# A single pair's projection on four array tiles, two fillers fewer, and the last output tile in two halves

## Chip, cores, metric

One core of one Trainium2 chip. The metric is the device time of one execution in microseconds (us). "us" of a record or a stretch is read from the profile of one execution; its clock starts with the span, which is some 1.7 us shorter than the device time.

## The reference, cut to what matters

```python
# q, k, v: (4, 8, 768, 64); proj: (64, 6)
q_bits = (einsum('bhsd,dk->bhsk', q, proj) > 0);  k_bits likewise
mask = bucket(q_bits)[:, :, :, None] == bucket(k_bits)[:, :, None, :]
scores = where(mask, q @ k.T / 8, -1e9);  attn = softmax(scores)
x = (attn @ v) laid out as (3072, 512)
out = (silu(x @ w_in)) @ w_out          # w_in (512, 2048), w_out (2048, 512)
```

The mask compares six sign bits of q and k. The kernel puts these bits, as extra rows of the contraction, under q and k, so that one matmul gives the score and, for unequal bits, a large negative term.

## The kernel before

Heads are worked in pairs. For pair 0 and pair 1 the projection (six random directions for each of q and k) is made for one pair alone; the later ones are made for two pairs at once, on the four 32-column tiles of the array.

```python
def proj_unit(*pairs):
    tiles = [(p, n) for p in pairs for n in range(2)]        # 2 tiles for one pair, 4 for two
    w = 32 * len(tiles)
    ...
    for c0, c1 in ((0, 512), (512, S)):
        for c, (p, n) in enumerate(tiles):
            nc.tensor.matmul(bp[32 * c : 32 * c + 32, 0 : c1 - c0], pw,
                             qk32[p][:, n * S + c0 : n * S + c1], start=True, stop=True)
    # VectorE: threshold to 0.5 or -0.5, one operation for each of the two banks

def bits_unit(pairs, i, par):      # VectorE: bits to where the scores' matmuls read them
    for n in range(2):             # q, then k: copies of 13 x 768, fp16
        ...
```

The start, with filler matmuls (`warm_up`) that keep TensorE busy while it would wait:

```python
t_unit(0, 0)
t_unit(0, 1, warm=4)       # 4 fillers between the transposes of q and of k
t_unit(0, 2)
warm_up(3)
cast_unit(0, 0)            # GpSimd: q and k to fp16 for the even head
cast_unit(0, 1)            # ScalarE: for the odd head
v_unit(0)                  # GpSimd: v of two heads to fp16, and its sums
proj_unit(0)
warm_up(9)
bits_unit((0,), 0, 0)      # for the even head (qka)
bits_unit((0,), 0, 1)      # for the odd head (qkb)
...
for p in range(NPAIR):
    plan(2 * NU * (p + 1) + 3, lambda p=p: x_unit(p))     # transposes of a pair's output
```

At the end, the second layer makes an output tile of 128 x 512 from 16 matmuls; VectorE halves it into SBUF and one transfer stores it:

```python
for ft in range(4 * part, 4 * part + 4):
    nc.tensor.matmul(o2[tt], g[ci][:, ft, ct * P : (ct + 1) * P], w_out16[:, ft, :], ...)
if part == 3:
    nc.vector.tensor_scalar(out=osb, in0=o2[tt], scalar1=0.5, scalar2=None, op0=ALU.mult)
    nc.sync.dma_start(out=dst[:, tt, :], in_=osb)
```

The softmax here doesn't subtract the row's maximum and nothing guards it: scores larger than these inputs give would overflow.

## Time and profile before

| | before |
|---|---|
| device time, median of 3 | 331.89 us |
| span of the profiled run | 330.2 us |
| TensorE busy, and its part of the chain that ended last | 98%, 90% |
| first projection (pair 0) on the chain | 1.51 us |
| first exponential of the scores | 12.40 us |
| last eviction, start | 326.52 us |

A chain line reads "start, duration, what": at each step the work that released the next one. The lines themselves are in the prediction below.

### The profile page before, as it was taken

What the parts mean: (1) busy time and instruction counts of PE and PEld (TensorE: products, weight loads), DVE (VectorE), ACT (ScalarE), POOL (GpSimd) and SP (SyncE); (2) the same over time, 40 slices, a digit from 0 to 9 for tenths busy, and PEclk for the clock granted to TensorE, in tenths of its full rate; (3) what the DMA queues carried; (4) which work ended last, traced back from release to release, by engine and by line L of the source; (5) the groups of instructions that cost most, each with busy time, mean ns of one, the idle gap of its engine ahead of it and who ended that gap; (6) DMA issues with size and microseconds to landing.
All of it is one profiled execution on the core that took longest, in us unless ns stands there. A gap on an engine that the chain in (4) does not pass through costs nothing.

```text
span 330.2 us, 7269 instructions
## 1 busy us (share of the span) xinstructions
PE 323.1 (98%) x2903; PEld 196.2 (59%) x2903; DVE 163.6 (50%) x335; ACT 226.6 (69%) x424; POOL 111.3 (34%) x177
## 2 busy tenths in 40 slices
PE   7999999999999999999999999999999999999995
PEld 4566645664786555665686655665576555448442
DVE  4586627348752181356953173345864222577311
ACT  2787989997996654897897645699798556267000
POOL 5689999329003570038303191034700000000000
PEclk9999999999999999999999999999999999999999
DMA  8999999960000381590000092220000010100021
GB/s 181 238 250 219 230 218 202 246 167 0 2 0 34 79 178 68 174 239 4 0 2 3 32 218 70 90 71 3 3 0 2 32 66 35 64 0 3 32 95 66
DMA packets 60259, 29.84 MB, mean 90 GB/s; under 512 B 50496, under 2 KB 56640, under 8 KB 60224
## 3 DMA queue, kind: packets, MB, share of 16 engines
q1 hardware_dynamic: 57472, 25.17, 31.8%
q0 software_dynamic: 2752, 4.20, 7.2%
q8 instruction: 23, 0.38, 0.5%
q14 instruction: 12, 0.10, 0.1%
HBM read 27.27 MB, written 6.29 MB: 102 GB/s over the span
## 4 chain that ended last, share of the span: by engine, by line
PE 90%; DVE 5%; ACT 2%; DMA 1%; issue 0%; ACTq 0%
PE o_ps L320 25%; PE h_ps L303 24%; PE s_ps L247 17%; PE o_ps L266 11%; PE tp_ps L162 6%; PE bp_ps L204 4%; DVE qka L224 2%; PE o_ps L261 2%; DMA q_sb<-in_q_dram 1%; PE xt_ps L286 1%; ACT u L250 1%; PE warm_ps L95 1%; DVE g L309 1%; DVE qkb L221 1%; DVE xT L288 1%; DVE qkb L224 1%
## 5 line engine op out<-in xcount | busy, mean ns | idle before, releaser
L250 ACT ACTIVATE u<-s_ps 128x512 f16<-128x512 f32 x288 | 160.2, 622 | 48.8 <-PE s_ps L247 48.4
L303 PE MATMUL h_ps<-xT,win 128*128 128x512 f16 (+1 forms) x512 | 95.3, 326 | 0.7 <-DVE xT L288 0.3
L266 PEld LDWEIGHTS <-u 128*128 128x128 f16 x1152 | 69.9, 97 | 42.4 <-ACT u L250 10.1
L320 PE MATMUL o_ps<-wout,g 128*128 128x512 f16 x384 | 94.4, 379 | 0.0
L309 DVE SCALAR_TENSOR_TENSOR g<-th,h_ps 128x512 f16<-128x512 f32 x96 | 65.7, 686 | 47.5 <-ACT th L307 47.3
L266 PE MATMUL o_ps<-vv,u 128*128 128x65 f16 x1152 | 82.4, 194 | 0.6 <-ACT u L250 0.3
L307 ACT ACTIVATE th<-h_ps 128x512 f32<-128x512 f32 x96 | 57.5, 599 | 24.9 <-PE h_ps L303 22.4
L303 PEld LDWEIGHTS <-win 128*128 128x128 f16 x512 | 49.5, 98 | 30.1 <-issue 3.0
L176 POOL TENSOR_SCALAR qka<-qk 64x1536 f16<-64x1536 f32 x16 | 23.4, 1463 | 118.5 <-ACT qk L166 115.0
L320 PEld LDWEIGHTS <-g 128*128 128x128 f16 x384 | 37.1, 98 | 35.6 <-issue 0.8
L247 PE MATMUL s_ps<-qkb 128*128 128x512 f16 x192 | 53.1, 326 | 0.0
L247 PE MATMUL s_ps<-qka 71*128 71x512 f16 x192 | 52.7, 327 | 0.0
L325 DVE TENSOR_SCALAR osb<-o_ps 128x512 f32<-128x512 f32 x24 | 16.6, 690 | 59.1 <-PE o_ps L320 59.1
L166 ACT COPY qk<-tp_ps 128x512 f32<-128x512 f32 x38 | 24.5, 645 | 5.4 <-PE tp_ps L162 5.4
L176 POOL TENSOR_SCALAR qkb<-qk 64x1536 f16<-64x1536 f32 x15 | 22.0, 1468 | 1.2
L275 DVE RECIPROCAL rec<-o_ps 128x6 f32<-128x6 f32 x32 | 6.1, 190 | 29.6 <-PE o_ps L266 29.6
L187 POOL TENSOR_TENSOR vsa<-v_sb 128x192 f32<-128x192 f32 x32 | 20.2, 632 | 0.0
L276 DVE TENSOR_TENSOR x_pr<-o_ps,rec 128x384 f16<-128x384 f32 x32 | 17.8, 557 | 1.1
L185 POOL CAST vv<-v_sb 128x384 f16<-128x384 f32 x32 | 17.8, 555 | 0.5
L224 DVE COPY qka<-bits 13x768 f16<-13x768 f16 x32 | 16.4, 514 | 0.7
L162 PE MATMUL tp_ps<-ident,q_sb 128*128 128x128 f32 x96 | 16.0, 279 | 0.4 <-DMA q_sb<-in_q_dram 0.4
L247 PEld LDWEIGHTS <-qka 71*128 71x128 f16 x192 | 15.5, 97 | 0.5 <-POOL vsb L189 0.3
(44 smaller groups left out, 189.8 us busy)
## 6 DMA issues: line engine op xcount, KB each, us to landing
q_sb<-in_q_dram SPq DMA_DIRECT2D x16, 384.0 KB, 6.5
k_sb<-in_k_dram SPq DMA_DIRECT2D x16, 384.0 KB, 6.9
v_sb<-in_v_dram SPq DMA_DIRECT2D x16, 384.0 KB, 5.3
out_dram<-osb SPq DMA_DIRECT2D x24, 256.0 KB, 2.0
win<-in_moe_w_in_dram POOLq DMA_DIRECT2D x4, 512.0 KB, 7.9
wout<-in_moe_w_out_dram POOLq DMA_DIRECT2D x4, 512.0 KB, 11.9
pw<-in_proj_dram POOLq DMA_DIRECT2D x2, 1.5 KB, 4.3
```

The lines of the kernel that those rows point to most:

```text
L162: nc.tensor.transpose(tp[:, j * P : (j + 1) * P], src[:, t].rearrange("p h d -> p (h d)"), ident)
L166: nc.scalar.copy(dst, tp)
L176: nc.gpsimd.tensor_scalar(out=dst[rows, :], in0=qk32[p][rows, :], scalar1=CS, scalar2=1.0, op0=ALU.mult, op1=ALU.mult)
L187: nc.gpsimd.tensor_tensor(out=sa, in0=src[:, 0:3], in1=src[:, 3:6], op=ALU.add)
L224: nc.vector.tensor_copy(out=dst, in_=bits[pairs][r, :])
L247: nc.tensor.matmul(sp[:, o0 : o0 + n], t[rows, S + jt * P : S + (jt + 1) * P], t[rows, c0 : c0 + n], start=True, stop=True)
L250: nc.scalar.activation(out=u, in_=sp, func=AF.Exp, scale=ESC)
L266: nc.tensor.matmul(o_ps[h][:, c0 // P + i, :], u[:, o0 + i * P : o0 + (i + 1) * P], vv[:, jt, :], start=False, stop=True, skip_group_check ...
L303: nc.tensor.matmul(hp[:, j, :], w_in16[dt][:, ft * P : (ft + 1) * P], xT[4 * b + dt][:, c0 : c0 + n], start=(dt == 0), stop=(dt == NDT - 1))
L307: nc.scalar.activation(out=th, in_=hp, func=AF.Tanh, scale=0.5)
L309: nc.vector.scalar_tensor_tensor(out=g[ci][:, grp * f : (grp + 1) * f, :], in0=th, scalar=1.0, in1=hp, op0=ALU.add, op1=ALU.mult)
L320: nc.tensor.matmul(o2[tt], g[ci][:, ft, ct * P : (ct + 1) * P], w_out16[:, ft, :], start=(ft == 0), stop=(ft == NFT - 1))
```

## The change

Its intent: spread the projection of a single pair over four array tiles (both halves of the sequence, for q and k), so that TensorE streams 384 columns instead of 768; take two fillers away ahead of k; and make the last output tile in two column halves, so that less is left to evict and to store behind the last matmul.

```diff
-        tiles = [(p, n) for p in pairs for n in range(2)]
-        chunks = ((0, 512), (512, S))
+        if len(pairs) == 1:
+            HS = S // 2
+            tiles = [(pairs[0], n, i * HS, i * HS, HS) for i in range(2) for n in range(2)]
+            chunks = [(0, HS, tiles)]
+        else: ...                        # two pairs: as before
 ...
     def bits_unit(pairs, i, par):
-        for n in range(2):               # 2 copies of 13 x 768
+        if len(pairs) == 1:              # 4 copies of 13 x 384
+            moves = [(2 * i + n, n, i * (S // 2), S // 2) for i in range(2) for n in range(2)]
+        else:
+            moves = [(2 * i + n, n, 0, S) for n in range(2)]
 ...
+        def mm2_last():
+            for i in range(2):
+                c = slice(i * DMODEL // 2, (i + 1) * DMODEL // 2)
+                op = ps.tile([P, DMODEL // 2], F32, tag="m", name="o2_ps", bufs=3)
+                for ft in range(NFT):
+                    nc.tensor.matmul(op, g[1][:, ft, P : 2 * P], w_out16[:, ft, c], ...)
+                ... # halve it, store it
 ...
-    t_unit(0, 1, warm=4)
+    t_unit(0, 1, warm=2)
```

More of the change, by code (lines that the diff above doesn't have):

```diff
@@ L194, in proj_unit @@
     def proj_unit(*pairs):
-        tiles = [(p, n) for p in pairs for n in range(2)]
-        w = 32 * len(tiles)
         bt = btp.tile([P, S], F16, tag="bits", name="bits")
-        chunks = ((0, 512), (512, S))
+        if len(pairs) == 1:
[3 more added lines that the diff above has]
+        else:
+            chunks = [(c0, n, [(p, m, 0, c0, n) for p in pairs for m in range(2)])
+                      for c0, n in ((0, 512), (512, S - 512))]
         bps = []
-        for c0, c1 in chunks:
+        for c0, w, tiles in chunks:
             bp = ps.tile([P, 512], F32, tag="m", name="bp_ps", bufs=3)
-            for c, (p, n) in enumerate(tiles):
-                nc.tensor.matmul(bp[32 * c : 32 * c + 32, 0 : c1 - c0], pw,
-                                 qk32[p][:, n * S + c0 : n * S + c1],
+            for c, (p, n, _, x0, w) in enumerate(tiles):
+                nc.tensor.matmul(bp[32 * c : 32 * c + 32, 0:w], pw,
+                                 qk32[p][:, n * S + x0 : n * S + x0 + w],
                                  start=True, stop=True)
             bps.append(bp)
-        for bp, (c0, c1) in zip(bps, chunks):
-            nc.vector.tensor_scalar(out=bt[0:w, c0:c1], in0=bp[0:w, 0 : c1 - c0],
-                                    scalar1=sc[0:w, 0:1], scalar2=sc[0:w, 1:2],
+        for bp, (c0, w, _) in zip(bps, chunks):
+            nc.vector.tensor_scalar(out=bt[:, c0 : c0 + w], in0=bp[:, 0:w],
+                                    scalar1=sc[:, 0:1], scalar2=sc[:, 1:2],
                                     op0=ALU.is_gt, op1=ALU.subtract)
@@ L215, in bits_unit @@
         p = pairs[i]
-        for n in range(2):
-            r = slice(32 * (2 * i + n), 32 * (2 * i + n) + NR)
-            t, r0 = ((QKA[p % NSL], 64), (QKB[p % NSL], 0))[par]
-            dst = t[r0 : r0 + NR, n * S : (n + 1) * S]
+        t, r0 = ((QKA[p % NSL], 64), (QKB[p % NSL], 0))[par]
+        if len(pairs) == 1:
+            moves = [(2 * i + n, n, i * (S // 2), S // 2) for i in range(2) for n in range(2)]
+        else:
+            moves = [(2 * i + n, n, 0, S) for n in range(2)]
+        for c, n, x0, w in moves:
+            r = slice(32 * c, 32 * c + NR)
+            dst = t[r0 : r0 + NR, n * S + x0 : n * S + x0 + w]
             if n == 1 and par == 1:
-                nc.vector.tensor_scalar(out=dst, in0=bits[pairs][r, :],
+                nc.vector.tensor_scalar(out=dst, in0=bits[pairs][r, 0:w],
                                         scalar1=sc[r, 2:3], scalar2=None, op0=ALU.mult)
             else:
-                nc.vector.tensor_copy(out=dst, in_=bits[pairs][r, :])
+                nc.vector.tensor_copy(out=dst, in_=bits[pairs][r, 0:w])
     NU = 9
@@ L313, in moe_units @@
         o2 = {}
+        def mm2_last():
[3 more added lines that the diff above has]
+                for ft in range(NFT):
+                    nc.tensor.matmul(op, g[1][:, ft, P : 2 * P], w_out16[:, ft, c],
+                                     start=(ft == 0), stop=(ft == NFT - 1))
+                osb = ops.tile([P, DMODEL // 2], F32, tag="osb", name="osb")
+                nc.vector.tensor_scalar(out=osb, in0=op, scalar1=0.5, scalar2=None,
+                                        op0=ALU.mult)
+                dst = out[b * S : (b + 1) * S, c].rearrange("(p t) n -> p t n", p=P)
+                nc.sync.dma_start(out=dst[:, NJ - 1, :], in_=osb)
         def mm2(tt, part):
@@ L334, in moe_units @@
         for tt in range(NJ):
+            if b == B - 1 and tt == NJ - 1:
+                units.append(mm2_last)
+                break
             for part in range(4):
```

## The prediction

> **What bounds the kernel now.** I read the page first, then the chain of waits over the first 21 us, then time-ordered views of the vector engine around the first projection and of the last 5 us. The page:
>
> ```profile
> PE 323.1 (98%) x2903; PEld 196.2 (59%) x2903; DVE 163.6 (50%) x335; ACT 226.6 (69%) x424; POOL 111.3 (34%) x177
> PEclk9999999999999999999999999999999999999999
> PE 90%; DVE 5%; ACT 2%; DMA 1%; issue 0%; ACTq 0%
> ```
>
> TensorE holds 90% of the chain that ended last and is busy 98% of the span, at full clock. So a change pays where it takes TensorE work off this chain, or shortens the two ends, where TensorE waits for a load or has nothing left to do. The chain from the start, in order of time (start us, us, what):
>
> ```profile
> 0.75 4.26 DMA q_sb<-in_q_dram
> 5.00 0.14 issue
> 5.14 1.28 PE tp_ps L162 x6
> 6.42 0.86 PE warm_ps L95 x4
> 7.28 0.65 PE tp_ps L162 x6
> 7.93 0.65 PE warm_ps L95 x3
> 8.58 1.51 PE bp_ps L204 x8
> 10.09 2.05 PE warm_ps L95 x9
> 12.13 0.24 PE s_ps L247
> ...
> 17.86 1.41 PE bp_ps L204 x8
> ```
>
> All three places of the change are on or next to it: four fillers between the transposes of q and k, the projection of pair 0, and that of pair 1. Note that 9 fillers follow the first projection: the first scores wait for them, not only for the bits. The vector engine there:
>
> ```profile
> 7.53 0.69 DVE L168 COPY qk<-tp_ps 128x512 f32<-128x512 f32 x1 [2.89 <-PE tp_ps L162]
> 9.69 1.25 DVE L209 TENSOR_SCALAR bits<-bp_ps,sc 64x512 f16<-64x512 f32 x2 [1.47 <-PE bp_ps L204]
> 10.98 0.86 DVE L224 COPY qka<-bits 13x768 f16<-13x768 f16 x2
> ```
>
> The bits that the first scores need are in place at 10.98 + 0.86 = 11.84, just before the fillers end at 12.13. The end of the kernel:
>
> ```profile
> 326.10 0.38 PE L320 MATMUL o_ps<-wout,g 128*128 128x512 f16 x1
> 326.52 0.69 DVE L325 TENSOR_SCALAR osb<-o_ps 128x512 f32<-128x512 f32 x1 [2.76 <-PE o_ps L320]
> 327.23 0.33 SPq L328 DMA_DIRECT2D out_dram<-osb  x1
> ```
>
> After the last matmul come 0.69 us of eviction and, from the issue at 327.23, 2.0 us to the landing (median of the output stores), all exposed.
>
> **What the Trainium skill says.** "TensorE: Matmul & The Clock Gate", section "Part 3: Packing small matmuls", says that matmuls on different 32-column strips of the array run concurrently, so that a pack costs about one matmul's duration plus some 4 ns per tile. The trace agrees: a projection of two pairs (four strips, 16 records) takes 1.43 us on the chain at 47.23, one of a single pair (two strips, 8 records) 1.41 us at 17.86. Two strips lie idle in the single one. "VectorE: DVE Perf Modes", section "The TRN2 errata", says that a VectorE instruction has a fixed cost besides its per-element time, so many small tiles pay it many times. The trace agrees: 802 ns for 512 columns and 527 for 256 in the same threshold operation give (802 - 527)/256 = 1.07 ns a column, so 527 - 275 = 252 ns fixed. "DMA: Bandwidth & Descriptors", section "Anatomy of one DMA", puts some 2.0 us of fixed setup and completion on a transfer (on another issue path); here the whole 256 KB store lands in 2.0 us, so the fixed part is smaller, but the split still shortens only the moving of the data.
>
> **The change part by part.**
>
> *Two fillers fewer ahead of k.* Four take 0.86 us, so two take 0.43 and TensorE would be free at 6.42 + 0.43 = 6.85. But the weight load of k's first transpose shows a wait of 0.18 us that ends with the landing of k, and it starts at 6.97. The chain has its transposes from 7.28, though the first one's record starts at 7.12 already (the chain counts only what follows the last filler's end). If it starts right after the weight load, as q's did (load 5.11, matmul 5.14), it starts at 7.00. So of the 0.43 us taken away, 0.12 at most is won, and none if the load needs its 0.14 us first. I take 0.07; k's landing takes the place of the fillers.
>
> *Projection of pair 0.* Before: the two strips run 512 columns, then 256, each in two passes (two records a matmul): 768 columns in 1.51 us. After: four strips run 384 columns at once. The stream is half as long. [...]The streaming part: a 512-column pass takes 0.43 us (the second pair of weight loads of this unit start 8.97, the third 9.39), so 768 columns in two passes take 0.43 x 2 x 1.5 = 1.29 us, and 384 take 0.64. Saved on TensorE 0.64 of 1.51, leaving about 0.87. The 9 fillers move up with it.
> The bits, meanwhile: the threshold can start only when the whole bank is done, some 0.9 to 1.0 us after the projection starts at 8.58 (now 1.1, behind the 512-column half), so at about 9.5; then one operation of 384 columns, 252 + 384 x 1.07 = 663 ns, in place of two that take 1.25 together: done at 10.2 instead of 10.94. Then four copies of 384 columns where there were two of 768. A plain copy of 768 took 0.36 (qkb) to 0.66 us (pair 1's qka); in pair 0 two took 0.86. If half of a 0.43 us copy is fixed, a copy of 384 takes 0.32, and the four 1.3 us, against 0.86. Bits in place at 11.5, three of the four (enough for the first score) at 11.2. The fillers end at 12.13 - 0.64 = 11.49. So the bits arrive about as the fillers end: the bound remains TensorE, with little room. I subtract 0.05 for this race. Pair 0: 0.64 - 0.05 = 0.59 us.
>
> *Projection of pair 1.* The same halving inside a stretch where TensorE is the bound and ScalarE waits for it (1.22 us idle before its exponential at 19.98): 1.41 becomes 0.77, 0.64 us saved. Its bits are needed only by the scores at 22.52, with qka's copies done at 20.20 + 1.33 = 21.53, about 1 us of room. The copies become four; at worst 0.45 us each, or 0.5 us more in all, the threshold gives 0.6 back, and the score comes 0.64 earlier relative to the projection's start. The room shrinks but holds.
>
> *Last output tile in halves.* 16 matmuls of 512 columns become 32 of 256. The weight loads double to 32, at 98 ns each in their record, and the 256-column matmuls of the first layer (272 ns a record, pipelined) show that this pace holds: in the stretch from 285.45 to 305.76, 64 of 512 and 64 of 256 take 20.3 us; with 0.216 a wide one, 64 x 0.216 = 13.8, leaving 6.5/64 = 0.10 a narrow one. So TensorE needs the same 3.45 us. The first half's eviction and store lie under the second half's 1.7 us of matmuls. The exposed eviction drops from 690 ns to 690 - 256 x 1.07 = about 420: 0.27 us. The exposed store is 128 KB instead of 256. Its data phase is estimated: the stores' data move at about 344 GB/s in the slice view of the last 5 us, so 128 KB less is 0.38 us; [...]I take 0.30. Sum 0.57.
>
> Sum: 0.07 + 0.59 + 0.64 + 0.57 = 1.87 us, 331.89 - 1.87 = 330.0.
>
> **The rivals.**
> *The early gain is swallowed later*, by a wait with its own clock. For: the DMA engines run at 80 to 90% until about 66 us, GpSimd at 90% from 16 to 41. Against: after the first q no load is on the chain; k of pair 1 is issued at 4.79 and used at 14.76, with 6.9 us the median to landing, 3 us of room. GpSimd's cast of pair 2 is done at 26.4, used at 33.6. If it came true, only the tail's 0.57 and something of the rest would stay: 331.0 or so.
> *The bits become the bound of the first scores.* For: twice as many copies, each with its fixed cost, beside GpSimd, and pair 1's copies of 768 took 0.66 each. If the four take 0.5 each, the bits come at 12.2 and nearly all of pair 0's 0.59 is gone: 330.6. Against: the copies of pair 0 averaged 0.43 and only three are needed.
> *Four strips at once don't keep up with single-pair data*, or the fewer fillers cost clock: speaking against, the two-pair unit at 1.43 us for four strips, and a removed span of 0.43 us of which TensorE idles only about 0.15, while 3 more fillers follow at once. A half-rate clock for 3 us would add some 1.5 us and cancel the gain: 331.5.
>
> **Range and chances.** The sure part is 0.64 + 0.57, so I'd be surprised above 331.0; with k early and a faster store it could reach 329.5. 8 in 10: 329.5 to 330.8. Over 2% would need 6.6 us, over three times all of it; slower by 2% would need a lost clock over tens of microseconds. Faster 0.01, same 0.98, slower 0.01.
>
> **What would show it.** In the changed profile: k's transposes start near 7.0 to 7.1 in the records with a short gap behind the fillers; the two single projections take 0.8 to 0.9 and 0.75 to 0.8 us on the chain; the first exponential starts at 11.6 to 11.8 instead of 12.40, and fillers, not bits, precede it; one 128x384 threshold takes about 0.66 us; from 21 us on everything lies 1.2 to 1.4 us earlier and the distance holds to the last layer; the last eviction takes about 0.42 us and the last store lands some 1.7 us after issue. It is wrong if the distance shrinks on the way, if the chain shows the vector engine ahead of the first scores, or if the clock drops.

## The result

| | before | after |
|---|---|---|
| median (lowest to highest), 6 runs each | 332.05 (331.83 to 332.36) | 331.64 (331.43 to 331.92) |
| ratio | | 0.9987, 95% interval 0.9974 to 1.0000 |
| span of the profiled run | 330.2 | 329.9 |

A ratio here is the mean time of one kernel's runs over that of the other's of the same rounds, so it isn't quite the ratio of the medians. 0.4 us came of the 1.87 that were predicted, and the interval reaches 1. The page of the changed kernel looks the same as before, with one hint in its line of the chain by engine: VectorE's part has grown.

```profile
PE 89%; DVE 6%; ACT 2%; DMA 2%; issue 1%; SPq 0%; ACTq 0%
```

The chain of waits of the changed kernel over the first scores (here and below, lines of "issue" of 0.05 us and less are left out of a chain):

```profile
7.03 0.87 PE tp_ps L162 x6
7.91 0.65 PE warm_ps L95 x3
8.55 0.91 PE bp_ps L209 x8
9.48 0.69 DVE bits L214
...
10.20 0.57 DVE qka L234
10.78 0.55 DVE qka L234
...
11.36 0.37 DVE qka L234
11.77 0.39 PE s_ps L257
```

The projection is down from 1.51 to 0.91 us as predicted. But behind it the chain has left the fillers and runs through VectorE: three copies of 384 columns take 0.57, 0.55 and 0.37 us. Before, two copies of 768 took 0.86 in all. Half as many columns made the single copy no shorter.

The same chain from the projection of pair 1 on:

```profile
17.64 0.83 PE bp_ps L209 x8
...
19.20 0.78 DVE qka L234
20.00 0.55 DVE qka L234
...
23.34 1.20 DVE qk L168 x2
24.54 0.11 DVE rec L285
24.68 0.57 DVE x_pr L286
25.29 0.51 PE xt_ps L296 x6
```

The projection takes 0.83 instead of 1.41 us. Then the chain stays on VectorE for 6.8 us: threshold, eight bit copies, two evictions of transposes, and the division of head 1 (x_pr). Only then can TensorE transpose pair 0's output (xt_ps). In the kernel before, the division (a line of the time-ordered view) was done at 24.24, and TensorE came to the transposes (a line of the chain) 1.4 us later:

```profile
23.68 0.56 DVE L276 TENSOR_TENSOR x_pr<-o_ps,rec 128x384 f16<-128x384 f32 x1
25.67 0.33 PE xt_ps L286 x6
```

The changed kernel's list of waits in the stretch from 20 to 28 us puts numbers to it: engine, line, what it waited for, us, times, longest.

```profile
ACT u L260 <- PE s_ps L257: 0.9, 1, 0.9
PEld L296 <- DVE x_pr L286: 0.7, 1, 0.7
PE xt_ps L296 <- DVE x_pr L286: 0.5, 1, 0.5
```

And the end, in order of time:

```profile
326.36 0.42 DVE L334 TENSOR_SCALAR osb<-o_ps 128x256 f32<-128x256 f32 x1 [1.32 <-PE o_ps L331]
326.81 0.33 SPq L337 DMA_DIRECT2D out_dram<-osb  x1
```

The last eviction is 0.27 us shorter (0.42 instead of 0.69), and the stores of 128 KB land 1.7 us after issue (2.0 before, for 256 KB). 326.81 + 1.7 = 328.51, and the span ends at 329.9: 1.4 us later. Before, 327.23 + 2.0 = 329.23 and 330.2: 1.0 us. So something like 0.4 us has appeared behind the landing.

To see where time goes without the noise of the launch, I cut each trace into stretches by the starts of records: from the first projection matmul to the first exponential of the scores, from that to the last such exponential, and from there to the start of the last record.

| kernel | projection to first exponential | first to last exponential | last exponential to end |
|---|---|---|---|
| before | 3.89 | 267.37 | 50.33 |
| after | 3.70 | 267.38 | 50.24 |

0.19 us won at pair 0 (0.59 predicted), nothing at pair 1 (0.64 predicted), 0.09 at the end (0.57 predicted). Over all runs below, a stretch that an edit doesn't touch repeats within 0.05 us; this is what makes parts of some tenths of a microsecond legible, while the device times scatter by a microsecond and more.

### The profile page after: what moved, and what is told of

The parts are those of the page before. It is cut to its first block, busy times and chain, and to the rows that moved or that the text cites. A ratio compares the mean times of both kernels' runs of the same rounds, so it can differ in the third digit from the quotient of the medians.

```text
span 329.9 us, 7309 instructions
## 1 busy us (share of the span) xinstructions
PE 321.7 (98%) x2917; PEld 196.4 (60%) x2917; DVE 166.5 (50%) x342; ACT 226.6 (69%) x424; POOL 111.0 (34%) x177
## 4 chain that ended last, share of the span: by engine, by line
PE 89%; DVE 6%; ACT 2%; DMA 2%; issue 1%; SPq 0%; ACTq 0%
PE o_ps L344 24%; PE h_ps L313 24%; PE s_ps L257 17%; PE o_ps L276 11%; PE tp_ps L162 6%; PE bp_ps L209 4%; DVE qka L234 2%; DMA k_sb<-in_k_dram 2%; PE o_ps L271 1%; ACT u L260 1%; PE xt_ps L296 1%; PE o_ps L331 1%; DVE g L319 1%; DVE qkb L231 1%; DVE qkb L234 1%; DVE xT L298 1%
## 5 line engine op out<-in xcount | busy, mean ns | idle before, releaser
L344 PE MATMUL o_ps<-wout,g 128*128 128x512 f16 x368 | 91.0, 379 | 0.0
L344 PEld LDWEIGHTS <-g 128*128 128x128 f16 x368 | 35.5, 98 | 33.7 <-issue 0.8
L349 DVE TENSOR_SCALAR osb<-o_ps 128x512 f32<-128x512 f32 x23 | 15.9, 690 | 56.3 <-PE o_ps L344 56.3
L234 DVE COPY qka<-bits 13x768 f16<-13x768 f16 (+1 forms) x36 | 17.9, 496 | 0.8
L162 PE MATMUL tp_ps<-ident,k_sb 128*128 128x128 f32 x96 | 15.6, 273 | 0.6 <-DMA k_sb<-in_k_dram 0.6
```

The lines of the kernel that those rows point to most:

```text
L162: nc.tensor.transpose(tp[:, j * P : (j + 1) * P], src[:, t].rearrange("p h d -> p (h d)"), ident)
L234: nc.vector.tensor_copy(out=dst, in_=bits[pairs][r, 0:w])
```

## The experiments

My theory had three parts. One: GpSimd's work beside the bit copies lengthens them, and the bits become the bound of the first scores. Two: the eight copies of pair 1 hold up VectorE's queue, and TensorE waits for the division behind them. Three: the end has closing waits (the last records of the sync engine, each a wait for two semaphores, the counters by which transfers and engines tell that they are done), and what they cost depends on which semaphore the last store uses. The rivals are in the expectations. Each run was timed in five rounds, with runs of the kernel before in between.

### One transfer more, nothing else

```diff
-        nc.sync.dma_start(
-            out=t, in_=v[b, h0 : h0 + 2].rearrange("h (p t) d -> p h (t d)", p=P))
+        for hh in ((0, 2),) if p != 12 else ((0, 1), (1, 2)):
+            nc.sync.dma_start(
+                out=t[:, hh[0] : hh[1]],
+                in_=v[b, h0 + hh[0] : h0 + hh[1]].rearrange("h (p t) d -> p h (t d)", p=P))
```

> The kernel before with one load (values of pair 12) issued as two transfers of half the size; nothing else. The transfers on the sync queue become 73 instead of 72, and the last store takes the first of the eight semaphores in turn instead of the eighth. Theory (closing waits): the sync engine waits for the eight semaphores in a fixed order at the end, some 0.06 us each, and seven of them now come after the landing of the last store, so 0.4 us is added at the end: about 332.4 against 332.0, and the profile shows the span longer by 0.4 us with the last store landing at the same time. Rival (the tail of the changed kernel lost its gain elsewhere, in the matmuls or the store): no change, within 0.1 us.

Measured: 332.50 us (332.16 to 332.65) against 331.71, ratio 1.0018 (1.0006 to 1.0030). The three stretches: 3.89, 267.34, 50.78. The last is 0.45 us longer than before, and nothing else moved. The rival has fallen: this kernel's last eviction and store are the old ones. The sync engine's records at the end show the mechanism. Each row is one closing wait, with the two semaphores named in it and the time on the profile's clock at which it was over; the left column is the kernel before, the right one the changed kernel:

```
before                               after
327.23 store, semaphore 118          326.81 store, semaphore 101
327.61 wait 113, 112                 327.19 wait 113, 112
327.68 wait 101, 111                 328.53 wait 101, 111   <- the last store has landed
327.75 wait 103, 110                 328.59 wait 103, 110
327.81 wait 104, 109                 328.66 wait 104, 109
327.87 wait 105, 108                 328.72 wait 105, 108
327.93 wait 114, 107                 328.78 wait 114, 107
328.00 wait 116, 106                 328.84 wait 116, 106
328.05 wait 117, 100                 328.90 wait 117, 100
329.26 wait 118, 115   <- landed     328.96 wait 118, 115
```

Eight semaphores serve the sync queue's transfers in turn. With 72 transfers the last one has the semaphore that is waited for last, and the other waits run while it is in flight. With 73 it has the first of the eight, and seven waits of some 0.06 us come after its landing: 328.96 - 328.53 = 0.43 us. The run with one transfer more shows the same in its own records: 329.55 - 329.12 = 0.43 us.

### The halves alone

The last output tile in two halves, as in the change, and nothing else (73 transfers).

> The kernel before with only the last output tile in two column halves (73 transfers). Theory (closing waits): eviction 0.27 us and store 0.31 us shorter, 0.43 us given back in the closing waits: 0.15 us faster, 331.9 against 332.05. Rival (the prediction's own sum): 0.58 us faster.

Measured: 331.64 us (331.59 to 332.35) against 331.71, ratio 1.0000 (0.9988 to 1.0013): the times can't tell 0.1 from 0. The stretches can: 3.89, 267.34, 50.24, so 0.10 us won and not 0.58.

### The halves with one load fewer

```diff
     def load_v(p):
         b, h0 = p // 4, 2 * (p % 4)
+        if p == 13:
+            return
+        if p == 12:
+            t = vld.tile([P, 4, NJ * D], F32, tag="ldv4", name="v_sb", bufs=1)
+            nc.sync.dma_start(
+                out=t, in_=v[b, h0 : h0 + 4].rearrange("h (p t) d -> p h (t d)", p=P))
+            v_sb[12], v_sb[13] = t[:, 0:2], t[:, 2:4]
+            return
```

> The same, and the values of pairs 12 and 13 loaded by one transfer instead of two, so that the transfers number 72 and the last half store has the eighth semaphore again. Theory (closing waits): the whole 0.58 us is there, 331.45 against 332.05, and 0.43 less than the kernel with the halves alone. Rival: the same time as with the halves alone.

Measured: 331.48 us (331.11 to 331.81) against 331.71, ratio 0.9989 (0.9977 to 1.0001). The stretches: 3.89, 267.32, 49.80. The end is 0.53 us shorter than before and 0.44 shorter than with the halves alone. So the prediction's 0.57 for eviction and store was there all along; a wait behind the landing ate it. The rival has fallen.

This run happened to show the fillers too. The clock of TensorE came up at 7.06 us (the trace's record of the granted clock; in the other runs between 4.36 and 6.94). Until then matmuls take about twice as long: in the kernel before, where it came up at 6.04, the first seven fillers took 3.15 us, the nine behind the projection 2.05. So here the four fillers ahead of k began at the low clock and took 1.17 us instead of 0.86. Chain of this run, with four fillers:

```profile
5.05 1.51 PE tp_ps L170 x6
6.57 1.17 PE warm_ps L103 x4
7.74 0.66 PE tp_ps L170 x6
```

### Pair 0 alone

The change's fillers and its four-tile projection for pair 0; pair 1 and the last tile as before.

```diff
-        if len(pairs) == 1:        # after, in proj_unit and in bits_unit
+        if pairs == (0,):
```

> The changed kernel with its two fillers fewer and its four-strip projection for pair 0 only; pair 1 in two strips and the last tile whole, as before. Theory (the copies of 384 columns are no shorter than those of 768 while GpSimd works, and the first scores wait for them): the first exponential at 12.2 instead of 12.4, 0.2 us faster in all. Rival (the prediction): the fillers are the bound, the first exponential at 11.7 to 11.8, 0.6 us faster.

Measured: 331.65 us (331.35 to 332.63) against 331.71, ratio 0.9999 (0.9986 to 1.0012): within the noise. The stretches: 3.70, 267.34, 50.32. So the 0.19 us at the first scores belong to pair 0, and no more than that; the first exponential stood at 12.15 us. The clock came up almost as late here (6.94), but with two fillers:

```profile
4.99 1.51 PE tp_ps L162 x6
6.50 0.71 PE warm_ps L95 x2
7.22 0.65 PE tp_ps L162 x6
```

The first transpose of k starts at 7.05 in its own record, against 7.57 with four fillers and the late clock. (k had landed at 6.71 and 6.61: TensorE came late in both.)

### Pair 1 alone

As the last, with `pairs == (1,)` and four fillers.

> The kernel before with the four-strip projection for pair 1 alone. Theory (vector engine queue): the projection is 0.6 us shorter, but eight bit copies instead of four hold up the vector engine, the division of head 1 comes late behind them, TensorE waits for it at the transposes of pair 0's output, and the stretch from the first exponential to the last stays at 267.3 us. Rival (the prediction): that stretch is 0.6 us shorter.

Measured: 331.86 us (331.61 to 332.65) against 332.03, ratio 0.9997 (0.9981 to 1.0014). The stretches: 3.89, 267.39, 50.33. The middle one stays at its 267.37. The exponentials show where the gain was and went: the 13th starts 6.95 us behind the first (7.58 before), so 0.63 us had been won there; the 25th starts 14.05 behind it (14.03 before), and it is gone.

### Pair 1 alone, transposes of pair 0's output later

```diff
-        plan(2 * NU * (p + 1) + 3, lambda p=p: x_unit(p))
+        plan(2 * NU * (p + 1) + (7 if p == 0 else 3), lambda p=p: x_unit(p))
```

> The same, with the transposes of pair 0's output planned four windows later (25 instead of 21), by when the vector engine has caught up. Theory (vector engine queue): the wait of TensorE before these transposes goes, and the stretch from the first exponential to the last becomes 266.7 us, 0.6 less. Rival (another bound in this stretch, ScalarE or a bank of the transposes waiting for its copy): it stays at 267.3.

Measured: 331.05 us (330.85 to 331.96) against 332.03, ratio 0.9976 (0.9958 to 0.9994). The stretches: 3.90, 266.73, 50.33. The 0.64 us of pair 1 are back in full. The wait for x_pr is missing from this run's list of waits; the transposes now follow TensorE's own work without a gap:

```profile
26.30 0.21 PE s_ps L258
26.52 0.34 PE xt_ps L297 x6
```

Nothing else bounds this stretch: the eight copies are as slow as before, but nobody waits for them.

### Pair 0, with GpSimd still during the copies

What spoke for GpSimd in the first place were its records in the changed kernel beside the copies:

```profile
10.15 0.51 POOL L185 CAST vv<-v_sb 128x384 f16<-128x384 f32 x1
10.62 0.59 POOL L187 TENSOR_TENSOR vsa<-v_sb 128x192 f32<-128x192 f32 x1
11.29 0.32 POOL L189 TENSOR_TENSOR vsb<-vsa 128x64 f32<-128x64 f32 x1
```

These end at 10.66, 11.21 and 11.61. The first three copies end at 10.77, 11.33 and 11.73: each 0.11 or 0.12 us after the GpSimd operation that ran when it was issued. (All sixteen bit operations of pairs 0 and 1 in this trace end 0.10 to 0.12 us after such an operation; in the kernel before, the six copies of 768 columns end 0.21 or 0.22 after.) The Trainium skill names a cause that fits, on a page that the prediction did not use: "SBUF — State Buffer", section "Who interferes with whom", says that VectorE and GpSimd share a pair of SBUF ports, that copies in the fast two-port modes need it, and that whoever issues first keeps it for the whole instruction. No trace names the mode of a copy or the port; what a run can show is whether GpSimd's work is the cause. The experiment, against the run of pair 0 alone:

```diff
-        if p == 0 and par == 1:        # cast_unit: which half ScalarE takes
+        if p == 0 and par == 0:
 ...
     cast_unit(0, 0)
-    cast_unit(0, 1)
-    v_unit(0)
+    v_unit(0, (0,))
     proj_unit(0)
     warm_up(9)
     bits_unit((0,), 0, 0)
+    hold = cst.tile([P, 1], F16, name="hold")
+    nc.gpsimd.tensor_copy(out=hold[64:77, :],
+                          in_=QKA[0][64:77, 2 * S - 1 : 2 * S])   # waits for the 4th copy
+    v_unit(0, (1,))
+    cast_unit(0, 1)
     bits_unit((0,), 0, 1)
```

> The changed kernel's pair 0 and fillers alone (as in the earlier run of these), with GpSimd kept still while the first four bit copies run: its values of head 0 are taken earlier, the cast of q and k for the even head goes to ScalarE, and a one-element operation that waits for the fourth copy goes ahead of the rest of GpSimd's work. Theory (GpSimd in the way of the copies): each of the four copies takes some 0.37 us, like those that ran beside GpSimd's small operations, the third is done before the fillers end, and from the start of the projection to the first exponential it takes 3.2 to 3.3 us instead of 3.70 (before: 3.89). Rival (a copy of 384 columns from one group of partitions to another takes 0.55 us by itself): the first two copies stay at 0.55 and the stretch at 3.70.

Measured: 331.19 us (331.01 to 332.67) against 332.03, ratio 0.9980 (0.9961 to 0.9999). The stretches: 3.25, 267.34, 50.35. The first is 0.64 us shorter than before: what the prediction had reckoned for the projection, without the 0.05 that it took off. In order of time on VectorE:

```profile
9.97 1.08 DVE L235 COPY qka<-bits 13x384 f16<-13x384 f16 x4
11.09 0.25 DVE L235 COPY qkb<-bits 13x384 f16<-13x384 f16 x1
...
11.69 0.45 DVE L235 COPY qkb<-bits 13x384 f16<-13x384 f16 x1
```

Four copies in 1.08 us, 0.25 each in the trace, less even than the 0.37 that I had expected (those had still waited behind small operations). The next plain copy after GpSimd goes on at 11.46 is at 0.45 again. The rival, a copy that is slow by itself, has fallen. On the chain the scores follow the fillers again, as the prediction had it:

```profile
9.20 2.05 PE warm_ps L95 x9
11.25 0.23 PE s_ps L258
```

### All three remedies with the whole change

The change, with GpSimd still, the transposes later, and one load fewer.

> The whole change with the three remedies together: GpSimd still during the first bit copies, the transposes of pair 0's output four windows later, and one load fewer so that the last store has the eighth semaphore. If the three theories hold, against the kernel before: 0.6 us at pair 0, 0.6 at pair 1, 0.53 at the end, and 0 to 0.4 from the fillers depending on when the clock comes up: 1.7 to 2.0 us faster, about 330.0. If one of them is wrong, its part is missing.

Measured: 329.88 us (329.82 to 329.96) against 332.03, ratio 0.9933 (0.9920 to 0.9947). The stretches: 3.25, 266.71, 49.79, so 0.64 + 0.66 + 0.54 = 1.84 us; the rest of the 2.15 between the medians lies ahead of the projection, which starts 0.26 us earlier in the profiled run (k's landing, the clock and the fillers differ from run to run), and in the scatter. Repeated:

> The change with the three remedies once more, as the standard for the next run: 329.9, 2.0 us under the kernel before.

Measured: 329.87 us (329.75 to 330.24) against 332.05, ratio 0.9936 (0.9923 to 0.9950), stretches 3.25, 266.69, 49.81. With the time taken out of the waits, the change gives what was predicted of it.

### The remedies without the change

GpSimd still and the transposes later, in the kernel before.

> The kernel before with the two remedies that touch its own work (GpSimd still during the first bit copies, the transposes of pair 0's output four windows later) and nothing of the change. Theory: in this kernel the fillers are the bound of the first scores and no one waits at the transposes, so both remedies bring nothing: 3.89 us, 267.3 us and 50.3 us for the three stretches, within 0.05. Rival (the remedies are gains by themselves): 0.4 and 0.6 us less.

Measured: 331.57 us (331.46 to 332.45) against 332.05, ratio 0.9991 (0.9977 to 1.0004). The stretches: 3.88, 267.33, 50.33, all as before. In the kernel before nobody waited at these places, so the remedies are no gains of their own. The median is 0.5 us lower, but the interval holds 1 and none of the three stretches carries it; this profiled run's k had merely landed early, and its first transpose stood at 6.64 us. The third remedy, one load fewer, was not tried without the change.

### The fillers alone

`warm=2` for `warm=4` in the kernel before.

> The kernel before with two fillers ahead of k instead of four, nothing else. Theory (the clock decides): the clock comes up at another moment in each run (4.4 to 7.1 us so far); with four fillers a late clock keeps k's transposes back (7.56 at a clock of 7.05), with two they start within 0.1 us of k's landing always. So 0 to 0.5 us, 0.1 to 0.2 on the mean, and the rest of the program as before: 3.89 from the projection to the first exponential, 267.3 to the last, 50.3 to the end. Rival (fewer fillers bring the clock up later): the transposes or the projection run longer than before.

Measured: 331.80 us (331.68 to 332.06) against 332.05, ratio 0.9993 (0.9980 to 1.0005): unclear by time, where 0.1 to 0.2 us was expected. The stretches: 3.89, 267.36, 50.34, untouched. The clock came up at 4.93 here, and transposes, fillers and projection ran no longer than elsewhere, so the rival found no support; but with an early clock two fillers gain nothing either. What they gain is shown only by the late clocks: k's first transpose at 7.57 with four fillers (clock at 7.06), at 7.05 with two (6.94); two more runs with two fillers and the clock at 6.3 to 6.5 had it at 6.79 and 6.86. That two fillers always let it start within 0.1 us of k's landing, as expected, had been contradicted already by the run of pair 0 alone: 7.05 with k landed at 6.71. How often the clock is that late, and so the mean gain, stays open.

### Seven fillers for nine

The mended kernel with `warm_up(7)` for `warm_up(9)` behind the first projection, to see whether the fillers bound the first scores again.

> The same with seven fillers behind the first projection instead of nine. Theory (with GpSimd still, the fillers are the bound of the first scores again; the third copy was done at about 10.76 and the fillers ended at 11.24): the first scores start at 10.8, 0.43 us earlier, and the projection to the first exponential takes 2.8 us instead of 3.25; 0.43 us faster, about 329.45. Rival (the bits or the sum of the values are the bound already): no gain; or the clock falls back: slower.

Measured: 329.62 us (329.55 to 329.70) against 332.05, ratio 0.9927 (0.9914 to 0.9939), and 0.25 us under the mended kernel. First stretch 3.04 instead of 3.25: 0.21 won, half of what I expected. The chain says why:

```profile
10.62 0.26 DVE qka L242
10.92 0.39 PE s_ps L265
```

The fillers were the bound, and with two fewer the bits are: the third copy ends at 10.88, and the scores follow. This is the fastest version measured, 2.4 us under the kernel before by the medians.

## Why the prediction was wrong, point by point

- **What bounds the kernel** was right: TensorE, and both ends. That the change would stay far within 2% was right too.
- **Fillers ahead of k**: 0.07 us expected. The profiled pair of traces gives 0.09 by k's first transpose (7.12 to 7.03 us, though k landed 0.07 later) and 0.03 by the start of the projection. So the size came out about right partly by luck: it depends on k's landing, which the prediction took from one trace, and on when the clock comes up, which it left out.
- **Projection of pair 0 on TensorE**: 0.64 us expected, 0.60 on the chain (1.51 to 0.91), right. The step that failed is "If half of a 0.43 us copy is fixed, a copy of 384 takes 0.32", with "the bits arrive about as the fillers end", for which 0.05 was taken off. The copies took 0.57, 0.55 and 0.37 us, and the race cost 0.45 (3.70 against 3.25 with GpSimd still). The rival "the bits become the bound of the first scores" was the one that came true, and even its figure (0.5 each) was close; it was given too little weight. A copy's duration was taken for a property of the copy. Alone, a copy of 384 columns takes 0.25 us, less than the 0.32 reckoned, and one of 768 takes 0.35 (the run of the remedies without the change). Beside GpSimd each copy waited until an operation of GpSimd was over, which was more than half of the first two copies' 0.57 and 0.55 us; so the time went with the number of copies, which the change doubles, and hardly with their length.
- **Projection of pair 1**: the 0.6 us was won on TensorE (the 13th exponential 0.63 us sooner), and given back. The step that failed is "The room shrinks but holds". It looked at one consumer of the bits, the scores, whose room did hold. The one that waited needs no bits at all: the division of head 1, which stands behind the eight copies in VectorE's queue, and through it the transposes on TensorE. The division had had 1.4 us of room; the eight bit copies took 4.1 us, where four had taken 2.2, and TensorE wanted its result 0.6 us sooner. That GpSimd lengthened these copies too (0.78, 0.55, 0.53 us) is likely, since they end 0.11 us after its operations as at pair 0, but no run kept it still at pair 1.
- **Last tile**: the sum of 0.57 us was right (0.53 once the closing waits lie before the landing), though the store's part partly by luck: the 0.30 came from 0.38 by a deduction that no run shows, and the landings differ by 0.31. The step that failed is one that isn't in the prediction: it let the end of the span follow the landing by a fixed time. A 73rd transfer moved the last store to a semaphore that is waited for early, and 0.43 us of waits went behind the landing.
- **The rival "early gain swallowed later, by a wait with its own clock"** put the blame on loads or GpSimd's casts. Swallowed it was, but by VectorE's queue; no load gave a wait in this stretch.
- **What would make it wrong** named two signs that came: "if the distance shrinks on the way", and "if the chain shows the vector engine ahead of the first scores".

So 1.87 us predicted less 0.4 at pair 0, 0.64 at pair 1 and 0.43 at the end leaves 0.4, and 0.41 lies between the medians. That these agree so closely is luck: the interval runs from 0 to 0.9 us, and the spans of the two profiled runs differ by 0.30. The parts rest on the stretches.

## What to carry to other kernels

When an operation is split into more and smaller ones, look at everything that stands behind them in the same engine's queue, not only at who needs their results, and check whether the duration you scale down is work or a wait for a neighbour: here it was paid once for each copy, and halving the columns didn't halve it. At the end of a kernel, read the closing waits and count the transfers: in this one, the last store should have the semaphore that is waited for last. A gain on the critical engine is real only as far as the next join; the stretches between fixed points of a trace show where it is lost.

## What the Trainium skill lacked or had wrong

- The closing waits are on no page that I found: nine waits of the sync engine of some 0.06 us each, in a fixed order, and 0.43 us more at the end if the last store has the first of the eight semaphores.
- "SBUF — State Buffer" fits what the runs show: bit operations of 13 x 384 beside a busy GpSimd took 0.36 to 0.78 us and ended 0.10 to 0.12 us after GpSimd's operation, and a copy took 0.25 beside a still one. What is lacking is a pointer to it in "VectorE: DVE Perf Modes", where a reader looks for the cost of a copy.
- "TensorE: Matmul & The Clock Gate" puts the change of the clock at some 4 us of matmuls, give or take 0.5. With the first matmul at 1.6 us, it came between 4.36 and 7.06 us in fourteen profiled runs, 2.8 to 5.5 us later: a spread of 2.7 us. The page's free-running window of about 3.4 us allows such a spread, but the earliest came sooner than one whole window after the first matmul.
- "DMA: Bandwidth & Descriptors" fits 2.0 us plus the bytes at 436 GB/s for another issue path. Here 256 KB landed in 2.0 us and 128 KB in 1.7, so by these two sizes the rate agrees (128 KB in some 0.3 us), and the fixed part is, by estimate from the page's rate, about 1.4.
